# A feed-forward block in bf16: the first transposing load cut to one contraction tile, and the early loads reordered over two queues

## The chip, the cores and the metric

The kernel runs on one core of a Trainium2 chip. The metric is the time of one execution on the device in microseconds; lower is better. Times given for a kernel are the median over its runs, and the profile is that of one execution.

## What is computed

```python
B, S, D, F = 1, 2048, 640, 1728      # x: [B,S,D]  w1: [D,F]  w2: [F,D], all bf16

def reference(x, w1, w2):
    h = jnp.einsum("bsd,df->bsf", x, w1)
    h = silu(h)
    out = jnp.einsum("bsf,fd->bsd", h, w2)
    return out
```

## The kernel before

The first product contracts over D = 640, that is five contraction tiles k = 0 to 4 of 128 rows. F = 1728 is cut into 13 column tiles ft of 128 (and a tail of 64), the 2048 tokens into four chunks of SCH = 512. A product of the first kind is always done in pairs: `step` (line 183) issues two matmuls of 64 output rows each, for the two halves of one ft, over 512 tokens, and `part` (line 189) is such a pair into the PSUM bank ft.

TensorE contracts over the partitions, so x has to lie in SBUF transposed: `xT` has the contraction tile in its second dimension. `turned(c0, c1, k0, k1)` (line 90) is a transposing load on SyncE's queue (SP) that brings the contraction tiles k0 to k1-1 of the tokens c0 to c1-1. `slab(eng, k, f0, f1)` (line 118) loads contraction tile k of w1 for the column tiles f0 to f1-1 on the queue of the engine given; without f0 and f1 it is the first NO = 8 column tiles (256 KB). NA = 5 divides slab 0: column tiles 0 to 4 (160 KB) and 5 to 7 (96 KB).

`early` (line 98) puts an instruction ahead of the barrier at the kernel's beginning, behind what `early` has already put there for the same engine. So for each engine the order of the calls of `early` is the order of issue. Before the change it is:

- SP: x tiles 0 and 1 in one load; slab 0's column tiles 5 to 7; slab 1; slab 2; x tile 2; slab 3; x tiles 3 and 4 in one load; slab 4; then the remaining columns of w1 in two loads (`ld_rest`, 320 KB, and `ld_rest2`, 560 KB). Behind them, after the barrier, come the 15 single-tile loads of the three later chunks of x (line 163), and w2.
- ScalarE: slab 0's column tiles 0 to 4, then the load of the activation table and one small Silu (`warm_up`, line 142).
- DVE and POOL: memsets of `z` and `warm`.
- TensorE: `first_dummies` (line 135), then `opening` (line 197).

`first_dummies` multiplies the zero tile `z` by itself into PSUM bank 3: 13 matmuls of 128 output rows by 256 columns, then one more in two halves of 64 rows. The results are overwritten later.

`opening` does the first chunk's first eight column tiles with the contraction outside and the eight banks inside: a sweep of eight pairs for k = 0, then for k = 1, 2 and 3 (`sweep`, line 192). The sweep of k = 0 waits for `ld_t[0]` and `ld_w1[0]`, and ahead of ft = 5 for `ld_w1b`; each later sweep waits for its `ld_w1[k]` and `ld_t[k]`. `ld_t[k]` is the semaphore point of the load that brings contraction tile k of x, so one load of two tiles is entered under both. The sweep of k = 4 stands after the barrier (line 208) and closes the banks one after the other, each followed by ScalarE's Silu into `hT`. Column tiles 8 to 12 of the first chunk follow (waits for `ld_rest`, and at ft = 10 for `ld_rest2`), then the other chunks, each behind a wait for its last load of x, then the tails and the second product.

Of the kernel before, what the change touches and what calls it, by code (L numbers as in the profile page):

```python
# [9 lines left out]
def bass_standalone__dense_activation_silu__prompt_kernel(  # L10
# [13 lines left out]
    P = 128  # L24
# [5 lines left out]
    SCH = 512  # L30
# [8 lines left out]
    pe, act, dve, pool, sp = nc.tensor, nc.scalar, nc.vector, nc.gpsimd, nc.sync  # L39

    with ExitStack() as es:
# [18 lines left out]
        def sem(name):  # L60
            s = es.enter_context(nc.semaphore(name))
            count[s.name if hasattr(s, "name") else name] = 0
            return [s, 0]

        def tick(ins, s, n=1):
            ins.then_inc(s[0], n)
            s[1] += n
            return (s, s[1])

        def wait(eng, *points):  # L70
            for pt in points:
                if pt is None:
                    continue
                s, v = pt
                key = (id(eng), id(s))
                if seen.get(key, 0) < v:
                    eng.wait_ge(s[0], v)
                    seen[key] = v
# [6 lines left out]
        def load(eng, out_ap, in_ap):  # L85
            s = sem(f"s_ld{n_dma[0]}")
            n_dma[0] += 1
            return tick(eng.dma_start(out=out_ap, in_=in_ap), s, 16)

        def turned(c0, c1, k0, k1):  # L90
            s = sem(f"s_tr{n_dma[0]}")
            n_dma[0] += 1
            return tick(sp.dma_start_transpose(
                out=xT[:, k0:k1, c0:c1], in_=xf[c0:c1, k0 * P:k1 * P]), s, 16)

        ET = mybir.EngineType

        def early(emit, engine, arrived=True):
            n = len(nc.main_func.blocks[0].instructions)
            r = emit()  # L100
            lst = nc.main_func.blocks[0].instructions
            new = lst[n:]
            del lst[n:]
            at = next(
                i for i, ins in enumerate(lst)
                if ins.opcode == ("EventSemaphore" if arrived else "Drain") and ins.engine == engine
            )
            lst[at:at] = new
            return r
# [4 lines left out]
        NO = NB  # L114
        NA = 5
        CO = NO * P

        def slab(eng, k, f0=0, f1=NO):
            return load(eng, w1s[:, k, f0 * P:f1 * P], w1_v[:, k, f0 * P:f1 * P])

        ld_w1 = {}
        ld_t = {}
        ld_t[0] = ld_t[1] = early(lambda: turned(0, SCH, 0, 2), ET.SP, False)
        ld_w1[0] = early(lambda: slab(act, 0, 0, NA), ET.Activation, False)
        p_z = early(lambda: tick(dve.memset(z[:, :], 0.0), s_dve), ET.DVE, False)  # L125

        bank_free = [None] * NB

        def dummies(n, w):
            for _ in range(n):  # L130
                for c0 in range(0, P, w):
                    pe.matmul(ps[c0:c0 + w, 3, 0:HB], lhsT=z[:, 0:w], rhs=z[:, :],  # L132
                              start=True, stop=True)

        def first_dummies():
            wait(pe, p_z)
            dummies(13, P)
            dummies(1, HC)

        p_warm = early(lambda: tick(pool.memset(warm[:, :], 0.0), s_pool), ET.Pool, False)  # L140
# [4 lines left out]

        early(warm_up, ET.Activation, False)

        ld_w1b = early(lambda: slab(sp, 0, NA, NO), ET.SP, False)
        ld_w1[1] = early(lambda: slab(sp, 1), ET.SP, False)
        ld_w1[2] = early(lambda: slab(sp, 2), ET.SP, False)  # L150
        ld_t[2] = early(lambda: turned(0, SCH, 2, 3), ET.SP, False)
        ld_w1[3] = early(lambda: slab(sp, 3), ET.SP, False)
        ld_t[3] = ld_t[4] = early(lambda: turned(0, SCH, 3, DT), ET.SP, False)
        ld_w1[4] = early(lambda: slab(sp, 4), ET.SP, False)
# [42 lines left out]
        def opening():  # L197
            first_dummies()
            wait(pe, ld_t[0], ld_w1[0])
            for ft in range(NO):  # L200
                if ft == NA:
                    wait(pe, ld_w1b)
                part(0, ft, 0, SCH, start=True)
            for k in range(1, DT - 1):
                sweep(k, 0, SCH, ld_w1[k], ld_t[k])
# [202 lines left out]
```

## Time and profile before

| | |
|---|---|
| median of 3 runs | 124.45 us (124.41 to 124.73) |
| span of the profiled execution, first to last instruction | 123.8 us |
| TensorE matmuls, busy | 121.3 us (98%) |
| line 175, first product: 540 matmuls | 59.6 us |
| line 175, second product, largest group: 376 matmuls | 46.0 us |
| line 132, dummies: 15 matmuls | 3.3 us |
| weight loads, busy (beside the matmuls) | 58.9 us |
| ScalarE busy | 38.8 us |
| HBM read, written | 4.51 MB, 2.62 MB |

The times are those of one profiled execution. A matmul's busy time is its record from start to modelled end, and neighbouring records overlap, so a mean of 384 ns for a matmul does not mean that one starts every 384 ns. In the groups and timelines the operand names stand as out<-in, and "L175" is line 175 of the kernel. "SPq" is the DMA queue of SyncE: its rows tell how long the issuing of a transfer took, not the transfer. The time from an issue to the landing of its data is listed with the issues.

### The profile page before, as it was taken

How to read it: one execution, taken by the hardware profiler on the slowest of the kernel's cores; microseconds unless marked ns; L12 is line 12 of the kernel's file. 1: busy time of each engine (PE TensorE's matmuls, PEld its weight loads, DVE VectorE, ACT ScalarE, POOL GpSimd, SP SyncE). 2: the span in 40 equal slices, each digit the busy share in tenths (PEclk: the TensorE clock that was granted, in tenths of full speed). 3: DMA queues.
4: the chain of work that ended last, by engine and by line, in shares of the span. 5: the costliest groups of instructions: out<-in, count | busy, mean ns of one | idle time of the engine just before them, and what ended most of it. 6: DMA issues, size and time to landing. Idle time of an engine off the chain costs nothing.

```text
span 123.8 us, 2298 instructions
## 1 busy us (share of the span) xinstructions
PE 121.3 (98%) x1056; PEld 58.9 (48%) x1057; DVE 6.9 (6%) x11; ACT 38.8 (31%) x67; POOL 0.3 (0%) x5
## 2 busy tenths in 40 slices
PE   8999999999999999999999999999999999999993
PEld 5345545545545545545544444444444444444452
DVE  0000000000000000000000022002200300222001
ACT  4000985555555555555530011001100200110110
POOL 0000000000000000000000000000000000000000
DMA  6999974554894000000000004302200220023112
GB/s 138 239 246 331 138 86 91 100 77 107 214 394 157 0 0 0 3 5 0 0 0 5 0 0 101 74 0 105 107 0 5 106 106 0 5 106 116 53 66 82
DMA packets 19625, 10.42 MB, mean 84 GB/s; under 512 B 13728, under 2 KB 19104, under 8 KB 19616
## 3 DMA queue, kind: packets, MB, share of 16 engines
q1 hardware_dynamic: 19472, 10.11, 34.1%
q10 hardware_dynamic: 144, 0.16, 0.6%
q8 instruction: 8, 0.13, 0.5%
q14 instruction: 1, 0.01, 0.0%
HBM read 4.51 MB, written 2.62 MB: 58 GB/s over the span
## 4 chain that ended last, share of the span: by engine, by line
PE 95%; DMA 3%; ACT 0%; issue 0%
PE ps L175 95%; DMA xT<-in_x_dram 3%; ACT o_sb L256 0%
## 5 line engine op out<-in xcount | busy, mean ns | idle before, releaser
L175 PE MATMUL ps<-xT,w1s 128*64 128x512 bf16 x540 | 59.6, 384 | 0.1
L175 PE MATMUL ps<-w2s,hT 64*128 64x512 bf16 (+3 forms) x376 | 46.0, 369 | 0.2 <-issue 0.2
L175 PEld LDWEIGHTS ps<-xT,w1s 128*64 128x64 bf16 x540 | 30.0, 111 | 29.6 <-issue 1.2
L179 ACT ACTIVATE hT<-ps 128x512 bf16<-128x512 f32 x52 | 30.0, 607 | 29.9 <-PE ps L175 29.9
L175 PEld LDWEIGHTS ps<-w2s,hT 64*128 64x128 bf16 (+1 forms) x377 | 21.0, 95 | 24.2 <-issue 0.2
L256 ACT CAST o_sb<-ps 128x512 bf16<-128x512 f32 (+1 forms) x9 | 5.0, 551 | 41.5 <-PE ps L175 41.5
L175 PE MATMUL ps<-hT,w2s 64*128 64x512 bf16 x104 | 11.7, 376 | 0.0
L175 PEld LDWEIGHTS ps<-hT,w2s 64*128 64x128 bf16 x104 | 5.0, 94 | 6.3 <-issue 0.4
L254 DVE CAST o_sb<-ps 128x512 bf16<-128x512 f32 (+1 forms) x8 | 5.4, 675 | 40.5 <-PE ps L175 40.5
L254 DVE CAST oT<-ps 128x512 bf16<-128x512 f32 x2 | 1.4, 692 | 74.2 <-PE ps L175 74.2
L256 ACT CAST oT<-ps 128x512 bf16<-128x512 f32 x2 | 1.2, 586 | 10.6 <-PE ps L175 10.6
L132 PE MATMUL ps<-z 128*128 128x256 bf16 (+1 forms) x15 | 3.3, 419 | 0.4 <-DVE z L125 0.4
L175 PE MATMUL ps<-w2t,hTt 64*128 64x512 bf16 (+2 forms) x17 | 2.9, 363 | 0.0
L132 PEld LDWEIGHTS ps<-z 128*128 128x128 bf16 (+1 forms) x15 | 1.9, 142 | 1.5 <-issue 0.4
L179 ACT ACTIVATE hTt<-ps 128x512 bf16<-128x512 f32 x2 | 1.2, 598 | 1.0 <-PE ps L175 1.0
L144 ACT ACT_TABLE_LOAD x1 | 1.3, 1283 | 0.5 <-issue 0.5
L175 PEld LDWEIGHTS ps<-w2t,hTt 64*128 64x128 bf16 x17 | 0.9, 94 | 1.1
L175 PE MATMUL ps<-hTt,w2t 64*128 64x512 bf16 x4 | 0.8, 376 | 0.0
L175 PEld LDWEIGHTS ps<-hTt,w2t 64*128 64x128 bf16 x4 | 0.2, 94 | 0.2
L144 ACT ACTIVATE warm<-warm 128x32 f32<-128x32 f32 x1 | 0.2, 229 | 0.0
L125 DVE MEMSET z<- 128x128 uint32 x1 | 0.2, 165 | 0.2 <-issue 0.2
L140 POOL MEMSET warm<- 128x32 f32 x1 | 0.1, 125 | 0.0
(4 smaller groups left out, 0.4 us busy)
## 6 DMA issues: line engine op xcount, KB each, us to landing
out_dram<-o_sb SPq DMA_DIRECT2D x15, 160.0 KB, 1.8
w2s<-in_w_dram SPq DMA_DIRECT2D x1, 1120.0 KB, 6.1
w1s<-in_w_dram SPq DMA_DIRECT2D x4, 256.0 KB, 4.1
w2s<-in_w_dram SPq DMA_DIRECT2D x1, 960.0 KB, 8.2
w1s<-in_w_dram SPq DMA_DIRECT2D x1, 560.0 KB, 7.0
w1s<-in_w_dram SPq DMA_DIRECT2D x1, 320.0 KB, 5.8
xT<-in_x_dram SPq DMA_TRANSPOSE x18, 3.7
w1s<-in_w_dram ACTq DMA_DIRECT2D x1, 160.0 KB, 2.7
```

Source lines behind the costliest of these rows:

```text
L125: p_z = early(lambda: tick(dve.memset(z[:, :], 0.0), s_dve), ET.DVE, False)
L132: pe.matmul(ps[c0:c0 + w, 3, 0:HB], lhsT=z[:, 0:w], rhs=z[:, :], start=True, stop=True)
L140: p_warm = early(lambda: tick(pool.memset(warm[:, :], 0.0), s_pool), ET.Pool, False)
L144: act.activation(out=warm[:, :], in_=warm[:, :], func=ACT.Silu)
L175: return pe.matmul(o, lhsT=l, rhs=r, start=start, stop=stop, skip_group_check=shared)
L179: r = tick(act.activation(out=out_ap, in_=in_ap, func=ACT.Silu), s_act)
L254: r = tick(dve.tensor_copy(out=out_ap, in_=in_ap), s_dve)
L256: r = tick(act.copy(out=out_ap, in_=in_ap), s_act)
```

## The change

Four things. The first transposing load brings x tile 0 alone. Slab 0's column tiles 5 to 7 move from SP's queue to ScalarE's, behind the first part and ahead of the activation table. On SP, slab 1 comes right behind the first load; then a load of the x tiles 1 and 2 together, which takes the place of the one of tile 2; then slabs 2 and 3, with nothing of x between them. The dummies of full width are 10 instead of 13.

```diff
-        ld_t[0] = ld_t[1] = early(lambda: turned(0, SCH, 0, 2), ET.SP, False)
+        ld_t[0] = early(lambda: turned(0, SCH, 0, 1), ET.SP, False)
         ld_w1[0] = early(lambda: slab(act, 0, 0, NA), ET.Activation, False)
+        ld_w1b = early(lambda: slab(act, 0, NA, NO), ET.Activation, False)
         p_z = early(lambda: tick(dve.memset(z[:, :], 0.0), s_dve), ET.DVE, False)
...
             wait(pe, p_z)
-            dummies(13, P)
+            dummies(10, P)
             dummies(1, HC)
...
         early(warm_up, ET.Activation, False)
 
-        ld_w1b = early(lambda: slab(sp, 0, NA, NO), ET.SP, False)
         ld_w1[1] = early(lambda: slab(sp, 1), ET.SP, False)
+        ld_t[1] = ld_t[2] = early(lambda: turned(0, SCH, 1, 3), ET.SP, False)
         ld_w1[2] = early(lambda: slab(sp, 2), ET.SP, False)
-        ld_t[2] = early(lambda: turned(0, SCH, 2, 3), ET.SP, False)
         ld_w1[3] = early(lambda: slab(sp, 3), ET.SP, False)
         ld_t[3] = ld_t[4] = early(lambda: turned(0, SCH, 3, DT), ET.SP, False)
```

The bytes loaded and the matmuls of the two products stay the same, as do all waits: each sweep still waits for its slab and its tile of x.

## The prediction

> **What bounds the kernel now.** I read the page first, then the chain of waits, then the first microseconds in order of time, then the transfers one by one.
>
> ```profile
> span 123.8 us, 2298 instructions
> PE 121.3 (98%) x1056; PEld 58.9 (48%) x1057; DVE 6.9 (6%) x11; ACT 38.8 (31%) x67; POOL 0.3 (0%) x5
> ```
>
> TensorE is busy for 98% of the span, so only a shift of its work, or a faster pace, can change the time. The chain of waits, in order of time, tells where it starts:
>
> ```profile
> 0.00 3.78 DMA xT<-in_x_dram
> 3.78 0.04 issue
> 3.82 106.78 PE ps L175 x706
> ```
>
> The first transposing load lands at 3.78 us. From 3.82 us to the end TensorE waits for nothing. If all later operands still arrive in time, what the first sweep gains is kept to the end. The timeline of the start, TensorE and its weight loads:
>
> ```profile
> 0.39 3.31 PE L132 MATMUL ps<-z 128*128 128x256 bf16 x15 [0.39 <-DVE z L125]
> 3.82 0.18 PEld L175 LDWEIGHTS ps<-xT,w1s 128*64 128x64 bf16 x4 [0.42 <-DMA xT<-in_x_dram]
> ...
> 5.53 0.18 PEld L175 LDWEIGHTS ps<-xT,w1s 128*64 128x64 bf16 x2 [0.25 <-DMA w1s<-in_w_dram]
> ```
>
> The 15 dummies fill 0.39 to 3.70 us; the first real weight load waited for the load of x. The line at 5.53 us is not a delay: its wait for the second part of slab 0 lasts 0.25 us, as the idle time between the neighbouring weight loads does, and that part landed at 5.24.
>
> The pace is not one pace. Two tables by stretch (PE busy, PEld busy, clock, DMA share, GB/s), the first of the matmuls of line 175 alone:
>
> ```profile
> 3.82:5.96 2.14, 2.14 (x12) 0.89 (x12) 1.00 1.11 296
> 6.30:8.46 2.16, 2.16 (x22) 1.10 (x20) 1.00 1.17 237
> ```
>
> The counts take in what touches an edge: 5 pairs of matmuls start in the first stretch and 10 in the second, so a pair (one ft) takes 0.427 us early and 0.216 us later, although the clock column reads 1.00 in both. A matmul lasts 634 ns early and 379 ns late. The pair that begins at 5.96 is followed by the next after 0.343 us, and dividing this between the two paces puts the change at 5.96 + 0.26 = 6.22 us. The rest of the kernel runs at the late pace.
>
> **The operands' slack now.** The transfers' times from issue to landing, added to their issue times, give the landings: the first load of x 3.78, slab 0's first part 2.86, its second part 5.24, slab 1 5.88, slab 2 6.59, x tile 2 7.15, slab 3 8.23, x tiles 3 and 4 9.24, slab 4 10.55, rest 12.51, rest2 14.14, the first later chunk of x 18.02. The sweeps of k = 0 to 4 begin at 3.82, 6.74, 8.46, 10.19 and 11.91 (8 pairs each), rest at 13.64, rest2 at 15.8, the next chunk at 19.0. The smallest slack is slab 1's: 6.74 - 5.88 = 0.86 us; the loads of x for k = 2 and k = 3 have 1.3 and 0.95, rest2 1.7, the chunk 1.0.
>
> **Part 1: the first load brings one tile.** Its issue on SP takes 1.33 us for two tiles; single tiles take 1.16 (tile 2) and 1.26 (later chunks), so the size hardly matters there. By the packet records the two-tile load sends 1024 packets of 256 B from 1.76 to 3.30 us and lands 0.48 us after its last. The 512th starts at 2.62. Half the load at this pace lands at 2.62 + 0.48 = 3.10. Single tiles on a quieter queue, in three stretches that hold one issue each (tile, then time to landing):
>
> ```profile
> xT<-in_x_dram SPq DMA_TRANSPOSE x1, 2.7
> ...
> xT<-in_x_dram SPq DMA_TRANSPOSE x1, 2.9
> ...
> xT<-in_x_dram SPq DMA_TRANSPOSE x1, 3.7
> ```
>
> They bound it: 2.74 at best, 3.7 as the median of all 18. I take 3.06, between the half load and the better single ones, since the first load finds an empty queue. TensorE starts 0.04 after the landing, at 3.10: 0.72 us earlier. Slab 0's first part (2.86) is there by then.
>
> What 0.72 us is worth depends on the pace. If it still changes at 6.22 us, the time from 3.10 to 6.22 holds 3.12 / 0.427 = 7.3 pairs, the other 0.7 pairs take 0.15, and k = 1 begins at 6.37 instead of 6.74: a gain of 0.36 us, which is 0.72 x (1 - 0.216 / 0.427). Half the earlier start is lost because it is spent at half pace.
>
> **Part 2: 13 dummies become 10.** One takes 0.213 us (2.28 to 2.50 to 2.71), so the dummies end 0.64 earlier, at 3.06 by the record's ends: the idle stretch before the first real matmul stays near the 0.12 us of now. They cover nothing else, and cost nothing as long as the load lands by then. Each 0.1 us of later landing costs 0.05 us of the gain.
>
> **Part 3: slab 0's second part on ScalarE.** It adds one issue of 0.37 us there (the first part's row); the table load and the warm-up behind it end near 2.4 instead of 2.05. Nothing waits for them: ScalarE's first Silu comes at 12.34, after 10.29 us idle. The part is now needed at 3.10 + 5 x 0.427 = 5.24 (its first weight load one pair earlier, 4.81). The first part took 2.7 us from its issue; this one, issued at 0.5, lands at 3.2 to 4.4 (0.5 + 3.9, its own row on SP). Cost nothing. What it can cost is bandwidth for the first load. Where the first part's packets run beside the load (1.7 to 2.35 us) the queues move 252 GB/s, and 224 where the load is alone (2.35 to 2.90): its packets slow the load by less than their own bytes.
>
> [...]
>
> **Part 4: SP's order.** SP loses one issue (0.56 us) and has T0, slab 1, tiles 1 and 2, slab 2, slab 3, then as before. By its rows slab 1 is issued at 1.3, tiles 1 and 2 at 1.95 (was 2.97 for tile 2), slab 2 at 3.2, slab 3 at 3.8, tiles 3 and 4 at 4.3, and everything behind, the later chunks of x too, about 0.5 earlier than now. New on the path: k = 1 (6.37) needs tiles 1 and 2. Bytes ahead of their end are T0, both parts of slab 0, slab 1 and themselves: 896 KB, or 917 kB. Adding up GB/s by stretch, the queues had moved 782 kB by 4.9 us and 972 by 5.4 now; 917 are reached at 5.25, and with 0.48 they land at 5.75: 0.6 us of slack. By the rows of issue to landing, 1.95 + 4.2 (tile 2) = 6.15 and 1.95 + 4.4 (tiles 3 and 4) = 6.35: just in time. A stall of the queues such as this one would then show:
>
> ```profile
> 3.40:3.90 0.50, 0.38 (x4) 0.08 (x6) 0.00 (x0) 0.00 (x0) 0.00 (x0) 1.00 0.56 46
> ```
>
> 46 GB/s for half a microsecond, right after the first load. It lies inside the 5.75 already. I take no stall, up to 0.8 (tiles 1 and 2 as late as tile 2 now, 7.15). Behind it slab 2 is due at 8.1 (about 7), tiles 3 and 4 at 9.8 (9.24 now, the same bytes ahead), rest at 13.3 (12.5), the next chunk at 18.6 (17.5): all hidden.
>
> **Sum.** The profiled execution spans 123.84 us and the median of the runs is 124.45, so 0.61 lies around the span. 123.84 - 0.36 = 123.48, with 0.61: 124.09, called 124.1. With the first load at 2.74 the gain is 0.51 (123.94); at 3.7 it is 0.04 (124.4).
>
> **Rivals.**
> A. The change of pace moves with the real work instead of standing at 6.22: then the whole 0.72 is gained, 123.73. For it: the early pace lasts 2.4 us after the first real matmul, and the records show no cause. Against: the dummies start at the same 0.39, and they are the same stream for TensorE.
> B. The single tile lands hardly sooner than two (3.5 to 3.8), as the median single tile does: TensorE idles after ten dummies, gain 0 to 0.15, 124.3 to 124.45. The change would not do what it says.
> C. Tiles 1 and 2 come late and k = 1 waits: the removed wait returns 2.5 us later. From 6.37 to 6.74 it eats the gain; at 7.15 the time is 124.45 + 0.45 = 124.9. For it: the stall above, and 1024 packets in one piece where tile 1 is already there now. Against: the count of bytes.
> D. The slower side: the early pace lasts longer because the idle stretch behind the shorter dummies lets TensorE fall back. If the 5.83 us from the first dummy to 6.22 count anew from 3.1, the change comes at 8.9: 2.7 us at 0.427 instead of 0.216 cost 1.34, less 0.36 gained, so 125.4. It decides from an idle stretch clearly above the 0.12 us of now, that is a first load after about 3.4. Against: the stretch does not grow if the load lands at 3.06.
> [...]
>
> **How the numbers follow.** Forecast 52%, A 12%, B 12%, C 13%, D 11%. A difference of 0.3% (0.37 us) is about what a measurement of this kernel tells from no change, so the forecast stands on the line: 28 of its 52 count as faster, 24 as no change. With A: faster 0.40. With B and 3 of C: no change 0.39. 10 of C and D: slower 0.21. The forecast's own range is 123.9 to 124.4. The range goes from A's 123.75 to C's end with a little above it, 125.0; D is left out with a little of A.
>
> **What would show it.** The first matmul of line 175 at 3.0 to 3.2; the pace changing near 6.2 with 7 pairs done; k = 1 starting near 6.4 with no idle ahead of it; issues of tiles 1 and 2 at 1.95 landing by 6.0; no new waits up to 19 us; the span near 123.5. A first matmul after 3.4, weight loads waiting for x after k = 0, or a change of pace away from 6.2 would prove me wrong.

## The result and the profile after

| | before | after |
|---|---|---|
| median | 124.56 us (124.41 to 124.83, 6 runs) | 126.09 us (124.90 to 126.93, 6 runs) |
| ratio after / before | | 1.0104, interval 1.0072 to 1.0136 |
| the same, measured again (e5 below; 25 and 10 runs) | 124.56 us | 125.28 us; 1.0065, interval 1.0038 to 1.0092 |

The change makes the kernel slower, by 0.7 to 1.0%, and scatters its runs over 2 us. The ratios leave out runs more than 1.5% above a kernel's fastest (here the one of 126.93 us); medians and ranges in this document are over all runs.

The profiled execution after has a span of 124.5 us. Its chain of waits begins so (start, duration, what):

```profile
0.00 3.64 DMA xT<-in_x_dram
3.64 0.04 issue
3.69 107.60 PE ps L175 x976
```

and its timeline (the dummies are line 133 now):

```profile
0.12 0.87 ACTq L88 DMA_DIRECT2D w1s<-in_w_dram  x2
...
0.39 2.67 PE L133 MATMUL ps<-z 128*128 128x256 bf16 x12 [0.39 <-DVE z L126]
...
3.69 0.19 PEld L175 LDWEIGHTS ps<-xT,w1s 128*64 128x64 bf16 x4 [0.92 <-DMA xT<-in_x_dram]
3.69 12.53 PE L175 MATMUL ps<-xT,w1s 128*64 128x512 bf16 x96 [0.63 <-DMA xT<-in_x_dram]
```

One tile lands at 3.64, 0.14 us before the two tiles of the kernel before. The dummies end at 3.06 by their records, so TensorE now stands idle for 0.63 us where it stood idle for 0.12. The pace, in two stretches of line 175 (PE busy, PEld busy, clock, DMA share, GB/s):

```profile
3.69:5.82 2.13, 2.13 (x11) 0.92 (x12) 1.00 1.13 242
7.85:10.00 2.15, 2.15 (x22) 1.12 (x20) 1.00 1.07 271
```

The same two paces, but the slow one lasts longer. The pair at 7.53 is followed by the next after 0.32 us, which puts the change of pace at 7.74 us; before it was 6.22. Nothing waits after 3.69. The two profiled spans differ by 0.67 us, and that is it: in the full pace both kernels run alike, and after reaches its eleventh pair at 7.85, before at 7.17.

The time around the span is not 0.61 us, as the prediction took it, but about 1.33 in the runs whose span is known (125.84 with 124.5 here; 123.99 with 122.6 for a run of before; the spans are listed to 0.1 us, and all lie at 1.26 to 1.42). By that the profiled execution of before, with 123.84, was an execution of about 125.17, slower than all six runs of the table. Its change of pace at 6.22 was a late one.

### The profile page after: what moved, and what is told of

Read it like the earlier page. It is cut to its first block, busy times and chain, and to the rows that moved or that the text cites. A ratio compares the mean times of both kernels' runs of the same rounds, so it can differ in the third digit from the quotient of the medians.

```text
span 124.5 us, 2292 instructions
## 1 busy us (share of the span) xinstructions
PE 121.5 (98%) x1053; PEld 59.5 (48%) x1054; DVE 6.9 (6%) x11; ACT 38.8 (31%) x67; POOL 0.3 (0%) x5
## 3 DMA queue, kind: packets, MB, share of 16 engines
HBM read 4.51 MB, written 2.62 MB: 57 GB/s over the span
## 4 chain that ended last, share of the span: by engine, by line
PE 95%; DMA 3%; ACT 0%; issue 0%
PE ps L175 95%; DMA xT<-in_x_dram 3%; ACT o_sb L256 0%
## 5 line engine op out<-in xcount | busy, mean ns | idle before, releaser
L175 PE MATMUL ps<-xT,w1s 128*64 128x512 bf16 x540 | 60.4, 388 | 0.6 <-DMA xT<-in_x_dram 0.6
L175 PEld LDWEIGHTS ps<-xT,w1s 128*64 128x64 bf16 x540 | 31.0, 112 | 29.9 <-issue 2.2
L133 PE MATMUL ps<-z 128*128 128x256 bf16 (+1 forms) x12 | 2.7, 419 | 0.4 <-DVE z L126 0.4
```

The source lines that it names most:

```text
L175: return pe.matmul(o, lhsT=l, rhs=r, start=start, stop=stop, skip_group_check=shared)
```

## The experiments

Each kernel ran beside the kernel before on the same chip; ratios are to that. Diffs are against the kernel before unless said otherwise.

**e1: thirteen dummies again**, against the changed kernel:

```diff
-            dummies(10, P)
+            dummies(13, P)
```

> The changed kernel with 13 dummies again. Theory I (the idle stretch behind the ten dummies, 0.63 us in the trace of after against 0.12 before, keeps TensorE at the early pace for longer: change of pace at 7.76 instead of 6.22 us): with the cover back the change of pace returns to about 6.2, the first real matmul stays at about 3.7, and the span falls from 124.5 to about 123.8. Rival II (the order of the transfers itself delays the pace or costs time): the change of pace stays after 7 us and the span near 124.5. A second question is the time around the span, 1.3 us in after against about 0.6 in before: if the transfers cause it, the run still takes about 125.1 here.

124.90 us (124.62 to 125.36), ratio 1.0044 (1.0018 to 1.0070). The changed kernel without its idle stretch is faster than with it, but still slower than before. In the profiled execution the change of pace came at 3.86, where about 6.2 was expected, and a new wait appears in the timeline of TensorE:

```profile
3.51 2.06 PE L175 MATMUL ps<-xT,w1s 128*64 128x512 bf16 x16
6.22 8.00 PE L175 MATMUL ps<-xT,w1s 128*64 128x512 bf16 x72 [0.65 <-DMA xT<-in_x_dram]
```

At the full pace the sweep of k = 0 has its 16 matmuls issued by 5.19. The sweep of k = 1 starts at 6.22, because tiles 1 and 2 land at 6.09. By the spacing of matmuls the gap is 0.8 us (1.03 instead of 0.22); the record, which counts to a modelled end, shows 0.65. So theory I is half right, and the order costs something too. The time around the span was 1.35 here, and as much for the runs of before: it is not an effect of the transfers, but my misreading.

**e2: ten dummies in the kernel before.**

```diff
-            dummies(13, P)
+            dummies(10, P)
```

> The kernel before with 10 dummies and nothing else changed. Theory I: TensorE idles 0.7 us ahead of the first real matmul (3.82), the change of pace comes 1 us or more later than 6.22 in at least part of the runs, the span grows by 0.5 to 1.5 us, and the runs scatter over 1 us or more. Rival II: the span stays at 123.8 to 124.0. The time around the span stays at 0.6 if the transfers cause its growth.

124.48 us (123.96 to 127.00), ratio 1.0004 (0.9974 to 1.0033). The expectation failed in the median and held in the tail: two of ten runs took 125.9 and 127.0. In the profile the load of two tiles landed at 3.36, TensorE idled 0.56 us by spacing, and the pace changed at 4.52 us. So a gap of half a microsecond did no harm in this launch, and the moment of the change is not fixed.

**e3: slab 0's second part on ScalarE, alone.**

```diff
         ld_w1[0] = early(lambda: slab(act, 0, 0, NA), ET.Activation, False)
+        ld_w1b = early(lambda: slab(act, 0, NA, NO), ET.Activation, False)
...
-        ld_w1b = early(lambda: slab(sp, 0, NA, NO), ET.SP, False)
```

> The kernel before with one edit: slab 0's second part on ScalarE's queue. If a second early transfer on ScalarE causes the time around the span to grow, the span stays at 123.6 to 124.0 and the run takes about 125.1; if not, 124.4. The landing of the first load of x tells what the shared engines cost it: 3.8 if nothing, up to 4.2 if the 96 KB go against it byte for byte.

124.51 us (124.31 to 127.22), ratio 1.0010 (0.9988 to 1.0032). The profiled execution is the longest run, 127.22:

```profile
4.35 0.18 PEld L175 LDWEIGHTS ps<-xT,w1s 128*64 128x64 bf16 x4 [0.94 <-DMA xT<-in_x_dram]
...
9.48 0.18 PEld L175 LDWEIGHTS ps<-xT,w1s 128*64 128x64 bf16 x2 [0.25 <-issue]
9.85 4.21 PEld L175 LDWEIGHTS ps<-xT,w1s 128*64 128x64 bf16 x40 [0.19 <-issue]
```

The first load landed at 4.31, 0.5 us or more later than in any trace with this part on SP and later than the 4.2 that the expectation allowed for its bytes (3.78 and 96 KB at the 252 GB/s of before, 0.39 us: an estimate). The profile of before counts SP's queue (q1) and ScalarE's (q10) alike as shares of the core's 16 DMA engines, 34.1% and 0.6%. Weight loads come in twos, 0.43 us apart, up to 9.48: the change of pace came at 9.80.

**e4: the changed loads of x, with that part on SP behind the first load; 13 dummies.**

```diff
-        ld_t[0] = ld_t[1] = early(lambda: turned(0, SCH, 0, 2), ET.SP, False)
+        ld_t[0] = early(lambda: turned(0, SCH, 0, 1), ET.SP, False)
...
         ld_w1[1] = early(lambda: slab(sp, 1), ET.SP, False)
+        ld_t[1] = ld_t[2] = early(lambda: turned(0, SCH, 1, 3), ET.SP, False)
         ld_w1[2] = early(lambda: slab(sp, 2), ET.SP, False)
-        ld_t[2] = early(lambda: turned(0, SCH, 2, 3), ET.SP, False)
```

> The changed order of the loads of x with 13 dummies, but slab 0's second part back on SP behind the first load. If the second part on ScalarE's queue delays the first load (3.64 in after), the first load lands at 3.1 here; if a single tile lands no sooner for another reason, at 3.5 to 3.7. If the second part on ScalarE causes the time around the span, it is 0.6 here and the run takes about 124.4; if the loads of x cause it, 1.3 and about 125.1.

124.64 us (124.49 to 124.81), ratio 1.0025 (1.0007 to 1.0044). The first load lands at 3.20. The runs lie within 0.32 us, and none comes near the 123.89 of before: k = 1 starts at 6.20, after the landing of tiles 1 and 2 at 6.06.

**e5: the changed kernel again**, with no edit.

> The changed kernel again, on the chip and beside the runs of this batch. [...] Rival IV (the change of pace stands at one time for one kernel): runs within 0.3 us of each other.

125.28 us (124.65 to 125.99): a spread of 1.3 us, so not one time for one kernel, and 0.81 us under the median of the first batch (126.09). In the profile the load landed at 3.47, the idle stretch was 0.67 us by spacing, and the pace changed at 5.33. The stretch was shorter than the 0.84 us by spacing of the first trace, and the change came earlier.

```profile
0.00 3.47 DMA xT<-in_x_dram
3.47 0.04 issue
3.52 106.55 PE ps L175 x976
```

**e6: the part on SP and ten dummies**, against e4:

```diff
-            dummies(13, P)
+            dummies(10, P)
```

> The changed order of the loads of x, with slab 0's second part on SP behind the first load and with 10 dummies. The first load should land near 3.2 as in the run with 13 dummies, so TensorE idles about 0.4 us. [...] If the count of dummies itself matters and not the idle time, about 126 as in after.

124.65 us (124.45 to 125.03), ratio 1.0014 (0.9992 to 1.0036). The first load lands at 3.03, TensorE idles 0.22 us, the pace changes at 4.00, and ten dummies are as good as thirteen (1.0014 against 1.0025 in e4). The first real matmul is 0.4 us earlier than with 13, and it gains nothing:

```profile
3.07 0.18 PEld L175 LDWEIGHTS ps<-xT,w1s 128*64 128x64 bf16 x4 [0.31 <-DMA xT<-in_x_dram]
...
3.07 2.35 PE L175 MATMUL ps<-xT,w1s 128*64 128x512 bf16 x16
6.11 8.22 PE L175 MATMUL ps<-xT,w1s 128*64 128x512 bf16 x72 [0.69 <-DMA xT<-in_x_dram]
```

k = 1 stands at 6.11 whether k = 0 began at 3.07 or 3.49.

**e7: tile 1 alone**, against e4:

```diff
-        ld_t[1] = ld_t[2] = early(lambda: turned(0, SCH, 1, 3), ET.SP, False)
+        ld_t[1] = early(lambda: turned(0, SCH, 1, 2), ET.SP, False)
         ld_w1[2] = early(lambda: slab(sp, 2), ET.SP, False)
+        ld_t[2] = early(lambda: turned(0, SCH, 2, 3), ET.SP, False)
```

> Tile 0, then slab 0's second part and slab 1 on SP, then tile 1 alone, slab 2, tile 2 alone; 13 dummies. If tiles 1 and 2 in one load are what holds k = 1 (6.2 in two traces, after 1.0 us of waiting), tile 1 alone lands at 5.3 to 5.6, k = 1 begins 0.6 to 0.9 earlier in launches with an early change of pace, and the median falls from 124.64 to about 124.2. If slab 1 or the queues as a whole hold it, the median stays at 124.6. The extra issue of 1.25 us on SP puts the later loads back and may bring a new wait at the second chunk of x.

125.06 us (124.72 to 125.30), ratio 1.0048 (1.0023 to 1.0073). Tile 1 landed at 5.51 and k = 1 started at 5.64, as expected; the median did not fall. The next loads are the bound at once:

```profile
5.64 3.80 PE L176 MATMUL ps<-xT,w1s 128*64 128x512 bf16 x32 [0.23 <-DMA xT<-in_x_dram]
10.25 4.08 PE L176 MATMUL ps<-xT,w1s 128*64 128x512 bf16 x36 [0.81 <-DMA xT<-in_x_dram]
```

With one more transposing issue on SP the tiles 3 and 4 landed at 10.12 (9.24 before, 9.52 after), and k = 3 waited.

**e8: seven dummies in the kernel before.**

```diff
-            dummies(13, P)
+            dummies(7, P)
```

> [...] If idle time doesn't set the pace: 124.3 as before.

125.69 us (125.22 to 126.21, 4 runs), ratio 1.0115 (1.0059 to 1.0171). With the transfers of before untouched, 1.27 us of idle time costs as much as the change does (1.0115 against 1.0104). Its profile has the change of pace at 6.71:

```profile
0.39 2.03 PE L132 MATMUL ps<-z 128*128 128x256 bf16 x9 [0.39 <-DVE z L125]
3.48 10.83 PE L175 MATMUL ps<-xT,w1s 128*64 128x512 bf16 x84 [1.06 <-DMA xT<-in_x_dram]
```

This shows that taking away dummies, and so leaving TensorE idle ahead of the first real matmul, makes the kernel slower by itself.

**e9, e10, e11: slab 0's second part on ScalarE behind the warm-up.** e9 is the changed kernel and e10 the kernel before with this one edit; e11 is e10 with the second edit and ten dummies. The part's load leaves its old place in all three.

```diff
         early(warm_up, ET.Activation, False)
+        ld_w1b = early(lambda: slab(act, 0, NA, NO), ET.Activation, False)
...
-        ld_t[0] = ld_t[1] = early(lambda: turned(0, SCH, 0, 2), ET.SP, False)
+        ld_t[0] = early(lambda: turned(0, SCH, 0, 1), ET.SP, False)
+        ld_t[1] = early(lambda: turned(0, SCH, 1, 2), ET.SP, False)
```

> The changed kernel, with ten dummies, but ScalarE issues slab 0's second part behind its warm-up (at 2.1 us instead of 0.5), when the first load's bytes are on their way. If those 96 KB are what put the first load from about 3.1 (three traces with the part on SP) to about 3.5 (three traces with it early on ScalarE), it lands at 3.0 to 3.2, TensorE idles under 0.4 us, and the runs lie between 124.4 and 125.0, median 124.7. If it's the use of ScalarE's queue itself, the load lands at 3.5 and the median is 125.3 to 126.0 as in after.

> The kernel before with slab 0's second part on ScalarE behind the warm-up. SP's later issues come 0.55 us earlier and the first load of two tiles isn't slowed (3.4 to 3.8). If slab 1 and the loads behind it hold back launches with an early change of pace, they land up to 0.5 us earlier and the median falls by 0.1 to 0.3 us; if nothing but the first load and the change of pace sets the time of before, it stays within 0.1 us.

> Tiles 0 and 1 in a load each, one behind the other, slab 0's second part on ScalarE behind the warm-up, the rest in the order of before, ten dummies. First load at 3.0 to 3.2 and first real matmul 0.4 us earlier than before; tile 1 by 4.5, so no wait at k = 1 but for slab 1. If the later loads (0.6 us later on SP than in the run with two tiles in one load) keep ahead of TensorE, the median is 0.1 to 0.3 us under before; if tiles 3 and 4 come after 9 us they hold k = 3 in launches with an early change of pace, and the time is that of before or up to 0.3 above.

Three misses: 125.39 us (ratio 1.0068, 1.0037 to 1.0099), 125.07 (1.0001, 0.9969 to 1.0032, but five of twelve runs over 126) and 125.93 (1.0114, 1.0082 to 1.0145). ScalarE's queue tells why, here of the first of them:

```profile
0.53 1.28 ACT L144 ACT_TABLE_LOAD   x1 [0.53 <-issue]
0.59 0.38 ACTq L88 DMA_DIRECT2D w1s<-in_w_dram  x1
1.82 0.23 ACT L144 ACTIVATE warm<-warm 128x32 f32<-128x32 f32 x1
```

The transfer, though behind both in the program, was issued at 0.59 us, beside the table load. So the part was no later than in the changed kernel, and the first loads landed at 3.52, 4.15 and 3.87. They are three more traces with the early part on ScalarE.

**e12, e13: the part held back by a real wait.** ScalarE waits for the end of its warm-up and issues at 2.1 us. e12 is e9, e13 is e10 with this edit.

```diff
-            act.activation(out=warm[:, :], in_=warm[:, :], func=ACT.Silu)
+            wait(act, tick(act.activation(out=warm[:, :], in_=warm[:, :], func=ACT.Silu), s_act))
```

> As the run before it with slab 0's second part behind the warm-up, but ScalarE now waits for its warm-up to end, so that the issue comes at about 2.1 us and not at 0.59. If the 96 KB beside the first load are what delays it, the first load lands at 3.0 to 3.2, TensorE idles about 0.3 us behind the ten dummies, the change of pace is not put off, and the median is 124.5 to 124.8. If ScalarE's queue as such delays it, the load lands near 3.5 and the median stays at 125.3 or above.

> The kernel before with slab 0's second part on ScalarE, issued at about 2.1 us behind the ended warm-up. The first load of two tiles lands at 3.4 to 3.8 as in before (not at 4.1 to 4.3 as with the early issue), the long runs of 126 to 127 us vanish, and with SP's later issues 0.55 us earlier the median is that of before or up to 0.3 us less.

In both, the first load lands as expected: 2.95 for one tile, 3.41 for two. The first's timeline:

```profile
2.09 0.35 ACTq L88 DMA_DIRECT2D w1s<-in_w_dram  x1
...
2.99 0.19 PEld L175 LDWEIGHTS ps<-xT,w1s 128*64 128x64 bf16 x4 [0.23 <-DMA xT<-in_x_dram]
```

So it is the part's early issue that delays the load, not the use of ScalarE's queue: issued at 0.59 us (e9) it goes with a landing at 3.52, issued at 2.09 (e12) with one at 2.95. The times missed. The first took 125.03 us (124.27 to 127.45, ratio 1.0034, 0.9999 to 1.0069), the second 125.35 (125.28 to 125.54, ratio 1.0073, 1.0049 to 1.0097). In the second the part comes too late: it lands at 6.21, behind slabs 1 and 2, and TensorE stops in the middle of k = 0:

```profile
3.49 1.34 PE L175 MATMUL ps<-xT,w1s 128*64 128x512 bf16 x10
6.26 7.96 PE L175 MATMUL ps<-xT,w1s 128*64 128x512 bf16 x72 [1.43 <-DMA w1s<-in_w_dram]
```

In the trace of the first, a run of 124.38 us, the part lands at 4.86 and holds nothing up; tiles 1 and 2 hold k = 1 by 0.2 us. Why its median missed, and why two of its runs took 126.9 and 127.5, the trace does not show.

**e14: the order of the changed kernel with the cut of before.**

```diff
-        ld_w1[2] = early(lambda: slab(sp, 2), ET.SP, False)
         ld_t[2] = early(lambda: turned(0, SCH, 2, 3), ET.SP, False)
+        ld_w1[2] = early(lambda: slab(sp, 2), ET.SP, False)
```

> The kernel before with one edit: the load of x tile 2 ahead of slab 2 instead of behind it, so that SP's order is that of the changed kernel and only the cut of the tiles into loads (0 and 1, 2) is that of before; 13 dummies, slab 0's second part on SP. If k = 1's wait for tiles 1 and 2 is what costs 0.25% in the run with tile 0 alone and 13 dummies, it's gone here and the median is that of before within 0.1 us. If the place of the transposing loads among the slabs costs it, the median is 0.2 to 0.4 us above before.

124.57 us (124.16 to 125.28), ratio 1.0012 (0.9984 to 1.0040). The fastest run is 0.33 us under the fastest of e4, and the profile has no stop at k = 1. But neither the median nor the interval separates it from e4 (1.0007 to 1.0044): that the coupling of tiles 1 and 2 costs the 0.25% is likely by the traces, not shown by the times. No version tried beats the kernel before.

## Why it went another way

Sixteen profiled executions, before and after among them, show how the parts act together. "Idle" is the time without a matmul streaming, from the spacing of starts (a dummy lasts 0.213 us so). The last column is the time from the start of the last packet of the first load, by the packet records, to its landing.

| slab 0's second part | tiles in first load | landed at, us | last packet to landing |
|---|---|---|---|
| on SP, or late on ScalarE | 1 | 3.20, 3.03, 3.03, 2.95 | 0.48 to 0.50 |
| early on ScalarE | 1 | 3.64, 3.46, 3.47, 3.52 | 0.95 to 0.98 |
| on SP, or late on ScalarE | 2 | 3.78, 3.36, 3.43, 3.46, 3.41 | 0.48 to 0.50 |
| early on ScalarE | 2 | 4.31, 4.15 | 0.86 to 0.99 |

(The sixteenth is e11: early on ScalarE, one tile with a second load right behind it, 3.87, and 1.40 from its last packet.)

*Part 1, a single tile lands at 3.06.* Right for the edit alone: 3.05 is the mean of the four traces without the part beside it, 0.44 under two tiles. *Part 3, "Cost nothing", is the step that failed.* The part costs the load 0.47 us (3.52 against 3.05), which takes back the whole 0.44 of the smaller load. The part's 96 KB make 0.39 us at the 252 GB/s of the prediction's row (an estimate), and the forecast's range had room for a landing at 3.7; I put that on the gain only, at half price, and not on the idle stretch. That was the second half of the same mistake.

*Part 2, the idle stretch "stays near the 0.12 us of now".* It became 0.63 by records, 0.84 by spacing. This is rival B bringing on rival D; I had priced them apart. D's sign and rough size were right (125.4; 126.09 and 125.28 measured) and the point from which it decides, a landing after about 3.4, was near (with ten dummies, a landing at 3.52 in e9 went with a change of pace at 5.31, one at 3.64 in after with 7.74); its chance of 11% was far too low, since it hung on the very landing that part 3 spoilt. Its reckoning was not right: counted anew, the change would have come at 8.9, and it came at 7.74 and 5.33. That its 125.4 lies so near the second median is luck.

*"If it still changes at 6.22 us" was wrong as a premise, and so was "0.61 lies around the span".* No run shows a change of pace that stands at one time: it came anywhere between 3.5 and 9.8 us in the sixteen traces, in the same kernel at 7.74 and at 5.33. With 1.33 us around it, the profiled execution of before is a late one, and its median run reaches the full pace about 0.6 / 0.494 = 1.2 us earlier, near 5.0 (an estimate). I had one draw and took it for the kernel. (The forecast's lower end, 123.94, had a slip of its own: it starts TensorE at 2.78, ahead of slab 0's first part at 2.86.)

*How first matmul, change of pace and stops make the time.* In the seven traces in which TensorE stops nowhere after its first real matmul (before, after, e2, e3, e8, e10, e11) the span is the time of that matmul, plus 0.494 times the time from there to the change of pace, plus 118.82 to 118.83 us, although the spans themselves reach from 122.78 to 125.87. So of after's 0.67 us over before, the later change of pace makes 0.75 (0.494 x 1.52), less 0.07 for the earlier start. What the other spans have above this sum are their stops: 0.98 us in e4, 1.15 in e6, 0.49 in e14.

What orders the sixteen traces is the idle stretch ahead of the first real matmul, by spacing:

| idle stretch, us | change of pace, us |
|---|---|
| 0.02 or less | 3.86 (e1); below 4 in e4, e7, e13, e14 |
| 0.15 to 0.33 | 5.02 (e12, 0.15), 4.00 (e6, 0.22), 6.22 (before, 0.33) |
| 0.56 to 0.71 | 4.52 (e2, 0.56), 5.33 (e5, 0.67), about 6.4 (e10, 0.70), 5.31 (e9, 0.71) |
| 0.84 to 1.27 | 7.74 (after, 0.84), 9.80 (e3, 0.86), about 8.2 (e11, 1.06), 6.71 (e8, 1.27) |

(The figures with "about" are estimates from start and span, by the sum above.) With up to 0.71 us of idle time the full pace was there by about 6.4, with 0.84 or more at 6.71 or later, and no trace lies between 0.71 and 0.84. After's first trace stands on the one side, its second (e5) on the other. Within a row the length does not decide: e8, with the longest stretch, has the earliest change of the last row. What sets the moment in a launch, no record shows.

Four traces (e2, e5, e9, e12) hold records of the granted clock. In them full clock begins at 4.51, 5.33, 5.31 and 5.02 us, within 0.02 us of where the spacing of the matmuls changes, and a record of half clock follows after the program's end. So in these four the change of pace is a change of the granted clock. Full clock lasts 119.466 us in all four, whenever it began.

The 31 runs of before that ran beside e1 to e4 spread over 1.33 us (123.89 to 125.22), the three other batches of before over 1.16 to 1.39 us. At half price, and if nothing else differs, 1.33 us would be a change of pace that moves by 1.33 / 0.494 = 2.7 us from launch to launch: an estimate, since before has one trace.

*Part 4, "I take no stall".* True of the late launch that I costed: in after's profile k = 1 finds tiles 1 and 2 (landed 6.17, forecast 5.75; the rows of issue to landing, 6.15 to 6.35, were the better estimate). In a launch with an early change of pace (e1, at 3.86) k = 0 ends by 5.4, and k = 1 stands until 6.22. This is rival C at another place than I had put it; with 13 dummies the two runs of this order stand at a ratio of 1.0025 (e4) and 1.0044 (e1). *Tiles 3 and 4, "the same bytes ahead",* landed at 9.52, later than before (9.24) although issued 0.47 us earlier; it is hidden in after's profile, and holds k = 3 in e6 by 0.24 us of spacing. Slab 2 (7.80, forecast about 7) and the next chunk (17.94, forecast 17.5) came later than forecast too, and were hidden.

Rival A fell: TensorE's change of pace does not follow the real work. The first real matmul starts at 3.48 in e8 and at 3.52 in e5, the change comes at 6.71 and 5.33; in e1, with 3.51, it comes at 3.86.

Of the slowdown, the cleanest pair is e5 and e6, run beside the same runs of before: moving the part back to SP, with the same ten dummies, takes the ratio from 1.0065 to 1.0014. Their intervals do not overlap (1.0038 to 1.0092, 0.9992 to 1.0036). Covering the idle stretch instead (e1) gives 1.0044, against 1.0104 and 1.0065 of the changed kernel beside other runs of before; its interval overlaps with that of e5, so the times alone do not show this step. What is left, up to 0.25% in e4, goes with the cut and order of the loads of x. The intervals do not divide it more finely.

## What to carry to other kernels

Where the start of a program has a fast and a slow pace, look at the spread of the runs before trusting one profile's moment of change: cost the edit for an early and for a late launch, for each has other waits. Filler work ahead of the first real work has to reach to the latest landing of what it covers, not to the expected one; here the three dummies saved left 0.84 us open, and the later change of pace cost after's trace 0.75 us, where the smaller load was to bring 0.36. And a small transfer moved to another queue is not free because that queue is idle: ask which landing it will be beside.

## What the runs showed of the hardware

The 96 KB beside a first load of one tile did not slow its packets: the last of 512 starts at 2.48 to 2.70 us with or without them. (With two tiles the last of 1024 starts at 3.28 and 3.33 with them, at 2.87 to 3.30 without.) What doubles is the time from the last packet to the landing, 0.48 to 0.50 us against 0.95 to 0.98. In after the part lands at 3.47 and the first load at 3.64, right behind it; in all seven traces with the early part the distance is 0.18 to 0.22 us. When the part is issued late (e12, at 2.09), the load lands first: the load at 2.95, the part at 4.86. What the landing waits for, no record shows.

In e9 ScalarE issued a transfer while its table load still ran (0.59 us in 0.53 to 1.81), so a place behind it in the program did not delay the transfer.

The clock column reads 1.00 at both paces, 0.427 and 0.216 us for a pair of matmuls. It is no measurement at the slow one: before's and after's traces hold no record of the clock at all, and e2's column reads 1.00 from 3 to 4 us, ahead of its first record at 4.51. The spacing of the matmuls shows the slow pace in every trace.
